# Fused attention and gated convolution FFN: convolution weights prepared at the start, the whole kernel in program order

## The chip, the cores and the metric

The kernel runs on one core of a Trainium2 chip. The metric is the device time of one execution in microseconds (us), the median over several executions. Engine names as in the profile: PE is TensorE (matmuls; PEld its weight loads), DVE is VectorE, ACT is ScalarE, POOL is GpSimd, SP is SyncE. The last two mostly issue transfers here.

## The reference

Eight batches, eight heads, 576 positions, head size 64. Linear attention with a root-mean-square norm, then an FFN whose hidden layer is gated by a convolution over the positions:

```python
kv  = einsum('bhsd,bhse->bhde', k, v)
out = einsum('bhsd,bhde->bhse', q, kv)
x   = out / sqrt(mean(out*out, -1) + 1e-6) * g_norm        # heads side by side: 512 columns
h   = maximum(x @ w_in, 0)                                 # 512 -> 1024
c[s] = cw[0]*h[s-1] + cw[1]*h[s] + cw[2]*h[s+1]            # per column of h, zero beyond the ends
y   = (h * sigmoid(c)) @ w_out                             # 1024 -> 512
```

The change concerns cw, the 3 x 1024 weights of the convolution (moe_conv_w).

## The kernel before

Batches are worked in five groups: batch 0, batch 1, and then three pairs. For each batch, k, v and q are loaded by POOL's queue as bf16, the first batch in two parts (six heads, two heads). For a batch, PE multiplies k by v (kv_mm, line 397) into a bank of PSUM; VectorE or ScalarE copies the result out (kv_out, line 351 or 349); q is transposed on PE (tr_mm, line 460) and copied out as qT; the product of qT and kv (line 371) gives `ot_ps`. ScalarE squares it, PE sums the squares (ss_mm, line 538), ScalarE takes Ln and Exp of the sums, PE spreads them over the columns (rb_mm, line 660 in the first group), and VectorE multiplies (x_mul, lines 671 and 678) to give xT. Then come `h` (line 785), the convolution and `o` (line 737).

The convolution is done in two ways. For the first group and some later parts it runs on PE with three diagonal matrices `diag` per column block (cw_diag, line 966, one VectorE instruction for each of the three taps). Elsewhere VectorE and ScalarE use weights relative to the middle tap, `cw_rel`, which cw_ratio (lines 973 to 980) makes in eight small VectorE instructions. Both start from `cw`: the 24 x 128 rows `cw_rows` come in by SP (line 286), PE transposes them in fp32 into `cw_ps` (cw_mm, line 959), VectorE copies them to `cw` (cw_out, line 962).

PSUM tiles come from two pools: three of two banks (`ps_two`) and two of one bank (`ps_one`). kv_ps, qT_ps, ss_ps and cw_ps, and at the start warm_ps and spread_ps, take turns in `ps_one`: each waits until the tile before the last has been read.

The order of the work has two parts. Everything ahead of the plan, lines 233 to 317, is put in order by a scheduler of the tile framework. The main part consists of numbered operations (class Plan), and the string ORDER lists them in the order in which they are issued; the letter behind a number chooses the engine (a is ScalarE, d is VectorE), and `*n` puts n filling matmuls of ones ahead of the operation (function `fill`, line 359) that keep PE running. This part runs under `tc.manual_schedule()` (line 1045), which keeps the order as written. Each engine works its queue strictly in order. The operations of kind LAND only stand for the time at which something is expected.

At the start PE runs warming matmuls of ones (line 242): `warm(14)` before the loads are issued, `warm(22)` behind the transposes that make `spread` (lines 301 to 306). `ident`, the identity matrix that transposes need, is made on POOL between the first transfer issues; `sel`, `neg`, `spread` and `spread32` are small constants for the sums and the spreading. The scheduler has put all 36 warming matmuls in one block ahead of the transposes, and the third load (q) between the two instructions that make ident.

Of the kernel before, what the change touches and what calls it, by code (L numbers as in the profile page):

```python
# [25 lines left out]
def _patch_pnc_remap() -> None:  # L26
# [28 lines left out]
FP32 = mybir.dt.float32  # L55
# [18 lines left out]
PARTS = (3, 1)  # L74
NORM_TABLES = "natural_log_exp_and_others"
ORDER = """
    103 8 11 0 7 17*7 18d 9 19*6 20a 24 21*2 29 25d 26 104 22 30d 27 31*4 32 12 10 34*1 35d 36*1 23a
    37d 33d 41*1 42 38*1 1 43*2 40d 105 13 39 49*2 50 28d 44 2 47*2 106*4 48 6 107a 108 53*2 45*2 54
    3 114*1 109*1 110a 115a 51*1 124 125a 46 119 120a 52 55 64 56a 4 5 65d 111 112 116 117 126 127
    113d 118d 205 212 217 68 128a 121 14 122 66 213d 218a 204 69d 123d 129 130 59 60d 222 82 131 67  # L80
    86 83a 87d 203 70 71 72 57 58 84 85 132 133 223a 134 135 209 210a 138 136 137 208 227 61 139
    228d 62 63 88 89 90 140 141a 148a 235 236d 144 145a 150a 206 146 240 147d 151d 142 143d 149d
    241a 211 214 216a 207 215 367 152 153 154d 157d 155d 156d 158 170 15 164 171a 165a 229 231a 219
    230 232 233a 234 168 169a 73 74d 172d 250 251d 77 78d 75 221a 245 16 159 220 175a 374 79 76 80
    246d 375d 174d 378 379d 81 160 166 167d 242 243 247 249a 248 365 366 94 252 224 173d 244d 176
    177 179d 181d 180d 178d 95a 237 238 225 253 100 101a 226d 382 383d 368 255 256 369 182 96 257 91
    371*1 372d 239a 254a 184 373 258*4 259 185 92a 272*2 273 268*2 269 264*2 265 262*1 263 186 370
    390*1 391a 162 93 260*1 266*1 161 183 386*1 267 270 271 261 97 98a 376 384 377 187 274 393 276
    387a 385 388 389 163 200 394a 288 275d 277d 290d 278 280 279d 289d 281d 201a 392 405 406d 401
    291d 402a 282 523 283a 284 285a 292d 525 532 533d 403 404 524 407 408 397 398d 286 544 545d 380  # L90
    526 527 287a 293d 294 295 296d 299d 298d 297d 300 528 399 400 381 529 530a 531 395 306 320 396
    409 410 411 316 307a 317a 548 549a 202 102 550 321a 412 413 414 415 308 309a 322d 314 315a 324d
    301 318 319d 325d 310 536 311a 551 552d 537d 312 313d 326 559 560a 323d 555*1 556d 327 330d 331d
    328d 329d 538 534 539 332 546 535 540 553 554 541a 561 547 562 194 563 564a 195a 196 99 542 543
    557 558 565 566 188 189a 418 416 567 568 417 336 304 335 424 419 569 425 302 197 303 420 421 190
    422 423 191 192a 193 430 431 428 429 432 433d 444 445a 570 426 427 440 334 305 434 435a 448d
    441a 436 437d 333 337 438 439a 449d 198a 199 446 447a 451d 442 443a 450a 452 453 454d 466 464
    465a 470 467a 471a 457d 455d 359 360a 456a 458 480d 476 477a 478 472 473a 479a 468 571 572 573
    361 469a 481d 483d 474 475a 484 575 482d 485 486d 362 350 462 363a 351a 364 352 459 353 354a 355
    576 577 578 586 579 489a 460 344 345a 461 487d 488d 490 574 590 584 587 591 341 342a 493 347  # L100
    348a 349 346 585 494 492 343 338 580 588 581 582 583 356 589 491 592 593a 598 599a 596 597a 463
    339a 340 600d 622 623a 603d 495 594 595a 604 601a 602d 605 608d 606d 607d 609d 610 646 618 620
    647a 621a 616 617a 624d 627d 619a 628 644 626d 645a 357a 625d 629 631d 630d 632d 613 633d 634
    611 640 358 641a 642 502 643a 614 503a 504 612 648d 650d 649d 615 652 651d 653 654d 656d 655d
    657d 658 520 666 521a 635 522 505 637 506a 507 667a 499 500a 501 517 678 664 638 636 639 665a
    518a 519 668d 669d 687 670 671 659 673d 508 679a 509a 660 672d 510 511 512d 513 661 674 514 662
    702 663 515a 516 680d 676 703a 681 704 682 683d 684 675 677 688a 690 689d 691 692d 696 693 697a
    685 698 699 686 700a 705 701 706d 707 694 695 496 497d 498 708 709a 710 711 717 712a 713 714
    718a 719 715a 716 720 721a 722
"""  # L110
NF = 4
GROUPS = ((0,), (1,), (2, 3), (4, 5), (6, 7))
# [82 lines left out]
def kernel(  # L195
# [11 lines left out]
    nc = tc.nc  # L207
# [3 lines left out]
    P = 128  # L211
# [5 lines left out]
    n_ff = D_ff // P  # L217
# [4 lines left out]
    consts = pool("consts", 1)  # L222
# [7 lines left out]
    ps_two = pool("ps_two", 3, space=PSUM)  # L230
    ps_one = pool("ps_one", 2, space=PSUM)

    nc.scalar.preload_act_table_set(NORM_TABLES)


    ones = consts.tile([P, 288], BF16, name="ones")
    nc.vector.memset(ones, 1.0)
    warm_ps = ps_one.tile([P, 288], FP32, name="warm_ps", tag="one")

    def warm(n):  # L240
        for _ in range(n):
            nc.tensor.matmul(warm_ps, ones[:, :P], ones, start=True, stop=True)  # L242

    warm(14)


# [12 lines left out]
    ident = consts.tile([P, P], BF16, name="ident")  # L259
# [17 lines left out]
    def load_w_out(half):  # L277
        fs = slice(half * n_ff // 2, (half + 1) * n_ff // 2)
        nc.gpsimd.dma_start(
            out=w_out_sb[:, fs, :], in_=moe_w_out.rearrange("(f p) m -> p f m", p=P)[:, fs, :])  # L280

    g_sb = consts.tile([P, 1], FP32, name="g_sb")
    for i in range(2):
        nc.sync.dma_start(out=g_sb[i * D:(i + 1) * D, :], in_=g_norm.unsqueeze(1))
    cw_rows = consts.tile([3 * n_ff, P], FP32, name="cw_rows")
    nc.sync.dma_start(out=cw_rows, in_=moe_conv_w.rearrange("k (f p) -> (k f) p", p=P))
    ident32 = consts.tile([3 * n_ff, 3 * n_ff], FP32, name="ident32")
    nc.vector.tensor_copy(ident32, ident[:3 * n_ff, :3 * n_ff])
    eps_sb = consts.tile([P, 1], FP32, name="eps_sb")
    nc.vector.memset(eps_sb, eps)  # L290

# [4 lines left out]
    for c in range(4):  # L296
        for i in range(2):
            nc.vector.memset(
                sel[i * D:(i + 1) * D, c, :24].rearrange("p (w m) -> p w m", m=8)[
                    :, :, 2 * c + i:2 * c + i + 1], 1.0)  # L300
    spread_ps = ps_one.tile([P, 4, P], BF16, name="spread_ps", tag="one")
    for c in range(4):
        for t in range(n_hd):
            nc.tensor.transpose(spread_ps[t * SM:(t + 1) * SM, c, :], sel[:, c, :], ident)
    spread = consts.tile([P, 4, P], BF16, name="spread")
    nc.vector.tensor_copy(spread, spread_ps)
    warm(22)

    spread32 = consts.tile([P, 2, P], FP32, name="spread32")
# [10 lines left out]
    plan = Plan()  # L320
# [3 lines left out]
    def ring(name, bufs):  # L324
        return rings.setdefault(name, Ring(bufs))


    TWO, ONE = ring("two", 3), ring("one", 2)
# [4 lines left out]
    def one_bank(shape, dtype, name):  # L333
        return ps_one.tile(shape, dtype, name=name, tag="one")
# [615 lines left out]
            g.o_ops.append(om)  # L950


    cw = consts.tile([P, 3, n_ff], FP32, name="cw")
    cw_rel = consts.tile([P, 3, n_ff], FP32, name="cw_rel")
    cst = {}

    def cw_mm():
        cst["ps"] = one_bank([P, 3 * n_ff], FP32, "cw_ps")
        nc.tensor.transpose(cst["ps"], cw_rows, ident32)

    def cw_out():
        nc.vector.tensor_copy(cw.rearrange("p k f -> p (k f)"), cst["ps"])

    def cw_diag(j):

        nc.vector.tensor_mul(
            diag[:, j, :, :], ident.unsqueeze(1).to_broadcast([P, n_ff, P]),
            cw[:, j, :].unsqueeze(2).to_broadcast([P, n_ff, P]))
# [10 lines left out]
        for j in (0, 2):  # L979
            nc.vector.tensor_mul(cw_rel[:, j, :], cw[:, j, :], sgn[:, 1, :])  # L980

    landed = plan.op("LAND", 9.0, None)
    mm = plan.op("PE", 0.3, cw_mm, deps=[landed])
    cw_done = plan.op("DVE", 0.2, cw_out, deps=[mm])
    Hold(ONE, mm, [cw_done])
    diag_done = []
    if any(map(any, C_PE)):
        diag = consts.tile([P, 3, n_ff, P], BF16, name="diag")
# [22 lines left out]
    for g in groups:  # L1011
        g.by_act, g.by_dma, g.x_from, g.kv_from = (c[g.n] for c in (BY_ACT, Q_DMA, X_FROM, KV_FROM))
        for b in g.bs:
            for name, src in (("k", k), ("v", v), ("q", q)):
                if b > 0:
                    need = []
                    if b > 1:
# [4 lines left out]
                        deps=[load_ops[name, b - 1]] if b > 1 else [])  # L1022
# [19 lines left out]
            tails([(groups[0], 0), (groups[1], 0)])  # L1042
    for g in groups:
        Hold(ring("h", 2), g.h0[0], g.o_ops)
    with tc.manual_schedule():
        for o in plan.order():
            if o.fn is not None:
                o.fn(*o.args)
# [1 line left out]
_INS = ['q', 'k', 'v', 'g_norm', 'moe_w_in', 'moe_conv_w', 'moe_w_out']  # L1050
_OUTS = [((8, 576, 512), 'float32')]
# [25 lines left out]
```

## Time and profile before

| what | value |
|---|---|
| time, median of 13 runs | 200.5 us (199.8 to 203.86) |
| the profiled execution's own time | 200.6 us |
| its span | 198.8 us |
| TensorE busy | 188.4 us (95%) |
| VectorE busy | 153.2 us (77%) |
| ScalarE busy | 139.1 us (70%) |
| transfers | 31.49 MB, mean 158 GB/s |

The profile is of one execution. The difference of 1.8 us between its time and its span lies around the instructions, before the first and after the last. Busy times are sums over one engine; the chain is followed back from the last instruction, at each step to the one that released it. The timeline gives instructions of an engine in order of time, merged where alike.

### The profile page before, as it was taken

To read this page: it belongs to the slowest core of one execution; us is meant where nothing else is said; L and a number is where in the kernel's file an instruction comes from. 1 tells how busy PE (TensorE), PEld (TensorE's weight loads), DVE (VectorE), ACT (ScalarE), POOL (GpSimd) and SP (SyncE) were. 2 spreads that over 40 slices of the span, in tenths; PEclk is the share of its full clock that TensorE was granted. 3 is DMA by queue.
4 is the path that set the end of the run, shared out by engine and by line. 5 is a ranking of instruction groups with operands and counts; after the bars stand their busy time and mean duration, and the time that the engine had idled before them with its cause. 6 is when DMAs were issued, how large, how long until landed. Compare 5 with 4: busy or idle time off the path is not lost.

```text
span 198.8 us, 4703 instructions
## 1 busy us (share of the span) xinstructions
PE 188.4 (95%) x1899; PEld 118.2 (59%) x1910; DVE 153.2 (77%) x281; ACT 139.1 (70%) x211; POOL 40.5 (20%) x61
## 2 busy tenths in 40 slices
PE   7999989999989989999999999999999999999990
PEld 4765566886854555777854477654457754644440
DVE  2127777897979866769999999999989999978200
ACT  2046068878969976288897998788988788677131
POOL 7706040013323114011000699110000000000000
PEclk9999999999999999999999999999999999999998
DMA  4999999997999999998689721398542034354653
GB/s 50 198 203 206 203 206 205 203 206 119 140 195 204 226 216 211 205 162 106 177 192 231 218 54 53 111 264 201 145 141 73 0 112 119 86 150 131 166 148 99
DMA packets 32714, 31.49 MB, mean 158 GB/s; under 512 B 2332, under 2 KB 28084, under 8 KB 32692
## 3 DMA queue, kind: packets, MB, share of 16 engines
q0 software_dynamic: 20976, 16.25, 53.9%
q1 hardware_dynamic: 11716, 14.93, 28.6%
q8 instruction: 15, 0.25, 0.5%
q14 instruction: 7, 0.06, 0.1%
HBM read 37.24 MB, written 9.73 MB: 236 GB/s over the span
## 4 chain that ended last, share of the span: by engine, by line
PE 70%; DVE 10%; DMA 9%; ACT 6%; issue 1%; POOL 0%; DVEq 0%; ACTq 0%
PE o_ps L737 27%; PE h_ps L785 20%; DMA v_sb<-in_v_dram 6%; PE ot_ps L371 4%; PE warm_ps L242 3%; DMA kv_sb<-kv_sb 3%; DVE tap L853 3%; PE qT_ps L460 3%; PE kv_ps L397 2%; PE c_ps L825 2%; DVE conv L875 2%; DVE conv L873 2%; PE rb_ps L660 2%; PE o_ps L928 2%; ACT qT L349 2%; DVE h L884 2%
## 5 line engine op out<-in xcount | busy, mean ns | idle before, releaser
L785 PE MATMUL h_ps<-xT,w_in_sb 128*128 128x288 bf16 x512 | 67.4, 286 | 0.4 <-DVE h L798 0.3
L737 PE MATMUL o_ps<-w_out_sb,h 128*128 128x512 bf16 x261 | 60.5, 379 | 0.6
L785 PEld LDWEIGHTS <-w_in_sb 128*128 128x128 bf16 x512 | 48.6, 98 | 15.0 <-issue 2.2
L737 PEld LDWEIGHTS <-h 128*128 128x128 bf16 x272 | 25.7, 98 | 30.6 <-issue 1.4
L879 ACT ACTIVATE conv<-conv,cw_rel 128x576 bf16<-128x576 bf16 (+1 forms) x40 | 37.1, 962 | 1.5 <-DVE conv L875 1.3
L796 ACT ACTIVATE h<-h_ps 128x576 bf16<-128x576 f32 x46 | 28.9, 648 | 8.4 <-PE h_ps L785 8.2
L853 DVE TENSOR_SCALAR tap<-h,cw_rel 128x576 bf16<-128x576 bf16 (+1 forms) x73 | 29.7, 449 | 2.4 <-ACT h L796 1.3
L349 ACT ACTIVATE o_sb<-o_ps 128x512 f32<-128x512 f32 x33 | 19.7, 596 | 15.5 <-PE o_ps L737 9.7
L483 ACT ACTIVATE sq<-ot_ps 128x576 bf16<-128x576 f32 x32 | 19.6, 655 | 4.2 <-PE ot_ps L371 3.7
L884 DVE TENSOR_TENSOR h<-h,conv 128x1152 bf16<-128x1152 bf16 (+3 forms) x16 | 22.0, 1380 | 0.6 <-ACT conv L834 0.5
L864 POOL COPY conv<-h 128x4 bf16<-128x4 bf16 (+3 forms) x12 | 3.9, 324 | 89.4 <-ACT h L796 31.6
L875 DVE TENSOR_TENSOR conv<-conv,tap 128x1152 bf16<-128x1152 bf16 (+11 forms) x36 | 20.4, 622 | 1.1
L873 DVE TENSOR_TENSOR conv<-h,tap 128x1152 bf16<-128x1152 bf16 (+11 forms) x36 | 20.3, 620 | 0.9 <-ACT tap L851 0.4
L349 ACT ACTIVATE qT<-qT_ps 128x576 bf16<-128x576 bf16 x14 | 8.8, 649 | 16.0 <-PE qT_ps L460 16.0
L798 DVE TENSOR_SCALAR h<-h_ps 128x576 bf16<-128x576 f32 x18 | 13.3, 753 | 5.4 <-PE o_ps L928 2.7
L371 PE MATMUL ot_ps<-qT,kv_sb 64*64 64x288 bf16 x192 | 12.4, 297 | 2.0 <-ACT qT L349 0.6
L678 DVE TENSOR_TENSOR xT<-o,rb_ps 128x576 bf16<-128x576 f32 x15 | 10.6, 750 | 3.7 <-PE rb_ps L663 2.0
L254 POOL DMA_DIRECT2D q_sb<-in_q_dram x9 | 6.8, 751 | 30.9 <-PE qT_ps L460 25.7
L684 DVE SCALAR_TENSOR_TENSOR xT<-ot_ps,g_sb,rb 128x576 bf16<-128x576 f32 x16 | 12.2, 811 | 1.1 <-PE ot_ps L371 0.8
L460 PE MATMUL qT_ps<-ident,q_sb 96*128 96x96 bf16 x192 | 12.6, 206 | 0.1
L460 PEld LDWEIGHTS <-q_sb 96*128 96x128 bf16 x192 | 10.4, 97 | 2.6 <-issue 0.8
L371 PEld LDWEIGHTS <-kv_sb 64*64 64x64 bf16 x192 | 5.1, 104 | 9.4 <-issue 7.6
(76 smaller groups left out, 173.1 us busy)
## 6 DMA issues: line engine op xcount, KB each, us to landing
out_dram<-o_sb SPq DMA_DIRECT2D x24, 192.0 KB, 2.3
rb<-scr SPq DMA_DIRECT2D x16, 288.0 KB, 5.3
k_sb<-in_k_dram POOLq DMA_DIRECT2D x7, 576.0 KB, 11.5
v_sb<-in_v_dram POOLq DMA_DIRECT2D x7, 576.0 KB, 13.7
q_sb<-in_q_dram POOLq DMA_DIRECT2D x7, 576.0 KB, 12.4
out_dram<-o_sb SPq DMA_DIRECT2D x24, 128.0 KB, 2.3
out_dram<-o_sb SPq DMA_DIRECT2D x24, 64.0 KB, 2.0
w_in_sb<-in_moe_w_in_dram POOLq DMA_DIRECT2D x2, 512.0 KB, 15.2
```

The source lines that it names most:

```text
L349: nc.scalar.activation(dst, src, AX.Copy, scale=1.0 if scale is None else scale)
L371: nc.tensor.matmul(ps[i * D:(i + 1) * D, e, :HS], kv, g.qT[bi][es, 2 * t + i, :], start=True, stop=True)
L460: nc.tensor.transpose(ps[:, i, j * PS:(j + 1) * PS], q_sb[:, 2 * t + i, j * P:(j + 1) * P], ident[:PS, :PS])
L483: nc.scalar.activation(g.sq[bi, t], ust["ps"][:, :, :HS], AX.Square)
L737: nc.tensor.matmul(st["ps"][:n, :], g.h[:, f, t0:t0 + n], w_out_sb[:, f, :], start=(f == 0), stop=(f == n_ff - 1))
L785: nc.tensor.matmul(ps[:, e, :HS], w_in_sb[:, t, f * P:(f + 1) * P], g.xT[:, t, at:at + HS], start=(t == 0), stop=(t == n_hd - 1))
L796: nc.scalar.activation(dst, st["ps"][:, :, :HS], AX.Relu)
L853: nc.vector.tensor_scalar_mul(dst, src, cw_rel[:, j, f:f + 1])
L873: nc.vector.tensor_add(c[:, :, here], h[:, :, here], t[:, :, there])
L875: nc.vector.tensor_add(c[:, :, there], c[:, :, there], t[:, :, here])
L879: nc.scalar.activation(cst["c"][:, f - f0, :], cst["c"][:, f - f0, :], AX.Sigmoid, scale=cw_rel[:, 1, f:f + 1])
L884: nc.vector.tensor_mul(hs, hs, cst["c"])
```

## The change

The plan's operations for cw are removed (the transpose of cw_rows and its copy), which lowers every later number in ORDER by two. The transpose and the copy now stand in the part ahead of the plan, behind the copy of `spread` and ahead of `warm(22)`. `manual_schedule()` is entered at the start, so that the part ahead of the plan is issued as written too: 14 warming matmuls, the transposes for spread, the transpose of cw_rows, 22 warming matmuls; and on POOL ident is made ahead of the third load. On SP cw_rows is loaded ahead of g_sb. `warm` takes a bank of its own each time it is called, which makes the second block wait for the copy of spread.

In ORDER the ratio (4) and the three diagonals (1, 2, 3) come first, ahead of the first kv_mm; before, they stood between the operations of the first group's norm. Otherwise the order is the same, and only numbers of fills differ: with the new operation numbers, 15 (first kv_mm) 7 to 6, 17 and 22 (first two transposes of q) 6 to 7 and 0 to 1, 19 and 29 (first and third product) 2 to 1 and 4 to 3, 32 (second kv_mm) 1 to 0, 34, 36 and 39 (transpose, sums of squares, fourth product) 1 to 2 each, 41 and 47 (rb, sums) 2 to 3 each, 51 and 43 (rb) 2 to 4 and 2 to 3, 112, 107 and 122 (transposes of batch 1) 1 to 2, 1 to 2 and 0 to 1; later 256 4 to 3, 262 2 to 1, 268 0 to 1, 369 and 553 1 to 0.

```diff
 ORDER = """
-    103 8 11 0 7 17*7 18d 9 19*6 20a 24 21*2 29 25d 26 104 22 30d 27 31*4 32 12 10 34*1 35d 36*1 23a
-    37d 33d 41*1 42 38*1 1 43*2 40d 105 13 39 49*2 50 28d 44 2 47*2 106*4 48 6 107a 108 53*2 45*2 54
-    3 114*1 109*1 110a 115a 51*1 124 125a 46 119 120a 52 55 64 56a 4 5 65d 111 112 116 117 126 127
+    0 4 1 2 3 101 6 9 5 15*6 16d 7 17*7 18a 22*1 19*1 27 23d 24 102 20 28d 25 29*3 30 10 8 32 33d
+    34*2 21a 35d 31d 39*2 40 36*2 41*3 38d 103 11 37 47*3 48 26d 42 45*2 104*4 46 105a 106 51*4 43*3
+    52 112*2 107*2 108a 113a 49*1 122*1 123a 44 117 118a 50 53 62 54a 63d 109 110 114 115 124 125
...
+    ctx.enter_context(tc.manual_schedule())
     nc.scalar.preload_act_table_set(NORM_TABLES)
...
-    warm_ps = ps_one.tile([P, 288], FP32, name="warm_ps", tag="one")
 
     def warm(n):
+        warm_ps = ps_one.tile([P, 288], FP32, name="warm_ps", tag="one")
         for _ in range(n):
             nc.tensor.matmul(warm_ps, ones[:, :P], ones, start=True, stop=True)
...
+    cw_rows = consts.tile([3 * n_ff, P], FP32, name="cw_rows")
+    nc.sync.dma_start(out=cw_rows, in_=moe_conv_w.rearrange("k (f p) -> (k f) p", p=P))
     g_sb = consts.tile([P, 1], FP32, name="g_sb")
     for i in range(2):
         nc.sync.dma_start(out=g_sb[i * D:(i + 1) * D, :], in_=g_norm.unsqueeze(1))
-    cw_rows = consts.tile([3 * n_ff, P], FP32, name="cw_rows")
-    nc.sync.dma_start(out=cw_rows, in_=moe_conv_w.rearrange("k (f p) -> (k f) p", p=P))
     ident32 = consts.tile([3 * n_ff, 3 * n_ff], FP32, name="ident32")
-    nc.vector.tensor_copy(ident32, ident[:3 * n_ff, :3 * n_ff])
...
+    nc.vector.tensor_copy(ident32, ident[:3 * n_ff, :3 * n_ff])
     spread_ps = ps_one.tile([P, 4, P], BF16, name="spread_ps", tag="one")
...
     nc.vector.tensor_copy(spread, spread_ps)
+
+    cw = consts.tile([P, 3, n_ff], FP32, name="cw")
+    cw_rel = consts.tile([P, 3, n_ff], FP32, name="cw_rel")
+    cw_ps = ps_one.tile([P, 3 * n_ff], FP32, name="cw_ps", tag="one")
+    nc.tensor.transpose(cw_ps, cw_rows, ident32)
+    nc.vector.tensor_copy(cw.rearrange("p k f -> p (k f)"), cw_ps)
     warm(22)
...
-    cw = consts.tile([P, 3, n_ff], FP32, name="cw")
-    cw_rel = consts.tile([P, 3, n_ff], FP32, name="cw_rel")
-    cst = {}
-
-    def cw_mm():
-        cst["ps"] = one_bank([P, 3 * n_ff], FP32, "cw_ps")
-        nc.tensor.transpose(cst["ps"], cw_rows, ident32)
-
-    def cw_out():
-        nc.vector.tensor_copy(cw.rearrange("p k f -> p (k f)"), cst["ps"])
...
-    landed = plan.op("LAND", 9.0, None)
-    mm = plan.op("PE", 0.3, cw_mm, deps=[landed])
-    cw_done = plan.op("DVE", 0.2, cw_out, deps=[mm])
-    Hold(ONE, mm, [cw_done])
+    cw_done = plan.op("LAND", 6.2, None)
...
-    with tc.manual_schedule():
-        for o in plan.order():
-            if o.fn is not None:
-                o.fn(*o.args)
+    for o in plan.order():
+        if o.fn is not None:
+            o.fn(*o.args)
```

## The prediction

> **What bounds the kernel now.** I read the page first (busy shares, chain by engine), then the timeline of the first 30 us, where all edits lie, then the chain piece by piece, to see what carries a delay from there to the end.
>
> ```profile
> span 198.8 us, 4703 instructions
> PE 188.4 (95%) x1899; PEld 118.2 (59%) x1910; DVE 153.2 (77%) x281; ACT 139.1 (70%) x211; POOL 40.5 (20%) x61
> PE 70%; DVE 10%; DMA 9%; ACT 6%; issue 1%; POOL 0%; DVEq 0%; ACTq 0%
> ```
>
> TensorE (PE) is busy for 95% and holds 70% of the chain. Little idle time is left in which a delay could vanish.
>
> Timeline, first part (start, duration, engine, line, operation; in brackets the idle time before and what ended it):
>
> ```profile
> 1.23 6.91 PE L242 MATMUL warm_ps<-ones 128*128 128x288 bf16 x36 [1.23 <-DVE eps_sb L290]
> 4.34 0.36 DVE L314 TENSOR_REDUCE neg<-ident 128x1 f32<-128x96 bf16 x2
> 8.06 0.41 PE L304 MATMUL spread_ps<-ident,sel 128*32 128x128 bf16 x16
> 8.52 0.42 DVE L306 COPY spread<-spread_ps 128x512 bf16<-128x512 bf16 x1 [3.82 <-PE spread_ps L304]
> 8.98 0.48 DVE L316 SCALAR_TENSOR_TENSOR spread<-spread,neg 128x256 f32<-128x256 bf16 x1
> 9.37 1.33 PE L397 MATMUL kv_ps<-v_sb,k_sb 96*64 96x64 bf16 x72
> 10.74 0.56 DVE L351 CAST kv_sb<-kv_ps 128x384 bf16<-128x384 f32 x1 [1.27 <-PE kv_ps L397]
> 11.37 0.68 PE L460 MATMUL qT_ps<-ident,q_sb 96*128 96x96 bf16 x12
> 12.53 0.32 PE L371 MATMUL ot_ps<-qT,kv_sb 64*64 64x288 bf16 x4 [0.24 <-ACT qT L349]
> ...
> 23.44 1.22 DVE L966 TENSOR_TENSOR diag<-ident,cw 128x1024 bf16<-128x1024 bf16 x1
> 26.63 2.35 DVE L966 TENSOR_TENSOR diag<-ident,cw 128x1024 bf16<-128x1024 bf16 x2
> ```
>
> To see here: all 36 warming matmuls run in one block, though the program has 14, then the transposes, then 22. VectorE (DVE) waits 1.27 us for kv_ps and then empties it at once, by 11.30. The two transposes of q run in one go at 11.37, the second in the bank that this copy freed.
>
> The chain, piece by piece (start, duration, work):
>
> ```profile
> 17.12 1.16 PE rb_ps L660 x4
> 18.29 0.35 PE ss_ps L359 x2
> 18.64 0.35 PE ss_ps L538 x2
> 18.99 0.35 PE rb_ps L359 x2
> 19.34 1.16 PE rb_ps L660 x4
> 20.50 0.54 PE kv_ps L359 x4
> 21.04 0.97 PE kv_ps L397 x48
> 22.01 0.35 PE rb_ps L359 x2
> 22.36 0.68 PE rb_ps L660 x2
> ```
>
> From 17.1 to 25.4 it is PE after PE, with no wait of another engine between. L359 is the fill: matmuls of ones, put in where PE was planned to wait. Here they are on the path: two cost 0.35, four cost 0.54, so one more costs about 0.12. After that the chain stays on PE up to 49.4, goes by a k/v swap (51.54, 6.42 us) and the load of v_sb (59.62, 11.59 us) to 71.25, and on over PE. The load and the swap start when PE lets their issuer go, so a delay at 27 us goes through.
>
> **The change part by part.**
>
> *1. VectorE's queue.* Moved ahead of the first kv copy: the copy of cw (0.18), eight small operations of the ratio (21.21 to 22.70 in the timeline: 1.5) and three diagonals (1.22 + 2.35 = 3.57). neg (0.36) and spread32 (0.48) now also stand behind the spread copy. When does this start? The 20 warming matmuls up to 6.0 us are 0.24 apart (4.77 us / 20), the later ones 0.12. So 14 end at 1.23 + 3.4 = 4.6; ident is ready by about 3.5, as its mask no longer stands behind a 0.73 us issue on POOL. The 16 transposes took 0.41 at the quick rate; I take 0.8 for the slow one: 5.4. Copy of spread (0.42) to 5.9, cw to 6.1, neg 6.5, spread32 7.0, ratio 8.5, diagonals 12.0. kv_ps is complete at about 10.8; its copy runs from 12.0 to 12.56 instead of 10.74 to 11.30: 1.26 late.
>
> Who waits: the second transpose of q, for the bank of kv_ps. It starts at 12.7 instead of about 11.7; the first product, behind it on PE, at 13.15 instead of 12.53 (+0.6); the copy of the second qT (0.46) ends at 13.66, the next product comes 0.6 late. Then fills fall away (4 to 3 before the third product, 1 to 0 before the second kv), others come in before the sums of squares (1 to 2), and the Ln and Exp on ScalarE are some 0.45 late: rb starts at 17.5 instead of 17.05. **+0.45.** Bounds: if the clock is up from 4.6 on, DVE is free at 11.6 and +0.15 is left. The landing of cw_rows isn't shown; it is issued first now, at 0.74. The nearest rows are g_sb on the same queue (2.3 us) and, far slower, the swaps (5.1): landed at 3.0 or 5.8. I take the first, as the load traffic has hardly begun; the second adds 0.4 and gives +0.85.
>
> *2. Warming in program order.* The cw transpose and the 22 warmers wait: the transpose for cw_rows (the warmers, kv_mm and all else of PE queue behind it), the warmers for the copy of spread, whose bank they reuse: PE stands for some 0.4 us around 5.5. Then 22 x 0.12 = 2.7 and 6 fills (7 before), with 0.25 between: kv_mm at 9.5 instead of 9.37. v lands at 2.23 + 6.9 = 9.1 and q at 3.10 + 8.2 = 11.3 either way (q's issue moves about 0.3 back behind the mask, but k and v, 864 KB at 200 GB/s, keep the queue full beyond it). Within the cover of q: **0**, if the clock rises at 6.0 as before; the first rival if not.
>
> The Trainium skill (TensorE: Matmul & The Clock Gate, "What's actually happening") says that the array runs at half clock until it was busy for a whole window of about 3.4 us, the window running freely. The rows agree on the two rates (0.24 and 0.12), not on when: 4.8 us after the first matmul, which a free window allows. By that rule a gap around 5.5 could cost one window more, to about 9.4, and by an estimate from it kv_mm would start near 11.3, +2.6 us in all with the terms below; by the rows taken above it is 0.
>
> *3. Fills, numbers changed.* Between rb (17.5) and the second transpose of batch 1 there are 6 more: 1 before the second ss, 2 and 1 before the rb of the last part, 1 each before two transposes; another before the first rb hides in its wait for Exp, and one before the third transpose in the wait for its bank. 6 x 0.12 = **+0.7**. Bounds: 0, if PE by then waits for ScalarE or VectorE after all, and 0.72. I take the upper, since the chain shows no wait there. Later net 3 fewer, two of them around 65 to 72, ahead of the wait for v_sb (cover: that load, 11.59), and one further on: **-0.1** (0 to -0.36).
>
> *4. Taken away.* cw_ps on PE (16.39, 0.24): the next rb waited for Exp until 17.05, so 0 (at most -0.24). On VectorE 5.2 us between 19 and 29: every xT there ends a wait for rb on PE (1.30, 0.37, 0.91 idle), and after the last two diagonals (to 28.98) h waits for h_ps until 29.07; only the first diagonal ends 0.1 past its rb. 0 (at most -0.1). The copies of qT, 4 on ScalarE at 25.45, stay as they are. g_sb lands about 0.6 later, still 10 us before its first reader at 14.9.
>
> Sum: 0.45 + 0.7 - 0.1 = +1.05, say **+1.1**. The profiled execution took 200.6 (198.8 span and 1.8 around it), 0.1 over the median of 200.5: **201.7**. By the ends of the bounds: 0.15 + 0 - 0.7 = -0.55 to 0.85 + 0.72 = +1.6, so 200.0 to 202.2 is the likeliest's own range.
>
> **The rivals.**
>
> *A. The clock rises late (slower).* For: the gap around 5.5 falls into the 4.77 us that before were unbroken. Against: most of that time is still filled. If the count began anew at 5.95, 20 warmers run 0.24 apart to 10.7, the other 2 and 6 fills take 1.0, kv_mm starts at 12.0 with the hand-over: +2.6 there; less 0.2 for fewer fills, plus 0.7 - 0.1: +3.0, **203.6**.
>
> *B. No difference.* The copy's delay is eaten by fills, and the added fills stand in real waits. For: the fills are counted from planned waits. Against: the chain above. +0.2: **200.8**.
>
> *C. Faster.* At 51.54 a swap of 32 KB takes 6.42 us among the loads of w_out, k and v, and v_sb 11.59 after it. If a shift of PE against POOL lets the swap land like a 64 KB store (2.0), up to 4.4 come free, of which PE can use its waits there (0.72 and 0.83) and some of the fills and slack before 71.25: I put 3.1. Net of +1.1 that is -2.0: **198.6**. It counts as faster once the swap saves 2.1. Against: its issue and the loads move together.
>
> **How the numbers follow.** Likeliest 0.45, A 0.25, B 0.13, C 0.17. A measurement tells about 0.5% (1.0 us) from no change, so the bounds are 199.5 and 201.5. The likeliest lies just above: 0.30 slower, 0.15 same. Slower 0.30 + 0.25 = 0.55; same 0.15 + 0.13 = 0.28; faster 0.17. Range: from 199.5 (C below it, some 0.1 after its weaker half) to 204.0, over A's price.
>
> **What would show it.** Spread transposes near 4.7 and VectorE in one block from about 5.5 to 12; the kv copy ending near 12.5 with no wait for PE; a gap on PE before the second transpose; the first h_mm at 28.0 instead of 26.95 and from there all stages 1.1 late. Wrong if: warming matmuls stay 0.24 apart beyond 7 us (A); h_mm of the first group at or before 27.2 (B); the first h_mm late but the v_sb wait at 71.25 over earlier than now (C).

## The result, and the profile after

The changed kernel takes 202.89 us (median of 11 runs, 202.34 to 205.84) against 200.4 us for the kernel before (median of 48 runs shown with it). The ratio is 1.014, with a 95% interval of 1.0111 to 1.0170: slower by about 2.5 us, where the prediction had +1.1. Some executions of most kernels here, of the one before too, take 1 to 4 us longer, with a mean granted clock of TensorE of 0.98 to 0.99; the ratios leave most of them out, and no reading below rests on one unless it says so.

The profiled execution of the changed kernel took 202.31 us, the lowest time seen; that of before took 200.6. So the two traces are 1.7 us apart and can account for that much of the 2.5; the rest lies in executions without a trace. The head of its page, with the chain by engine:

```profile
span 200.5 us, 4719 instructions
PE 189.0 (94%) x1905; PEld 118.5 (59%) x1916; DVE 153.9 (77%) x281; ACT 139.0 (69%) x211; POOL 40.6 (20%) x61
PE 64%; DMA 14%; DVE 10%; ACT 5%; POOL 2%; issue 2%; SPq 0%; DVEq 0%; ACTq 0%; POOLq 0%
```

PE's share of the chain fell from 70% to 64%, and the transfers' rose from 9% to 14%. So something that PE waits for got later. The timeline of the changed kernel (start, duration, engine, line, operation, in brackets the idle time before and what ended it) shows where:

```profile
1.23 3.41 PE L243 MATMUL warm_ps<-ones 128*128 128x288 bf16 x14 [1.23 <-DVE eps_sb L290]
4.57 0.41 PE L305 MATMUL spread_ps<-ident,sel 128*32 128x128 bf16 x16
5.03 0.42 DVE L307 COPY spread<-spread_ps 128x512 bf16<-128x512 bf16 x1 [1.30 <-PE spread_ps L305]
5.50 2.85 PE L243 MATMUL warm_ps<-ones 128*128 128x288 bf16 x22 [0.36 <-DVE spread L307]
8.30 3.49 DVE L962 TENSOR_TENSOR diag<-ident,cw 128x1024 bf16<-128x1024 bf16 x3
10.35 1.33 PE L404 MATMUL kv_ps<-v_sb,k_sb 96*64 96x64 bf16 x72 [1.26 <-DMA v_sb<-in_v_dram]
11.72 0.56 DVE L358 CAST kv_sb<-kv_ps 128x384 bf16<-128x384 f32 x1
13.70 0.32 PE L378 MATMUL ot_ps<-qT,kv_sb 64*64 64x288 bf16 x4 [0.23 <-ACT qT L356]
...
18.45 1.23 PE L667 MATMUL rb_ps<-rs,spread 32*128 32x288 f32 x4
...
29.09 2.12 PE L792 MATMUL h_ps<-xT,w_in_sb 128*128 128x288 bf16 x16
```

The last two of these in the kernel before:

```profile
17.05 1.23 PE L660 MATMUL rb_ps<-rs,spread 32*128 32x288 f32 x4
26.95 2.12 PE L785 MATMUL h_ps<-xT,w_in_sb 128*128 128x288 bf16 x16
```

TensorE is ready for the first kv_mm at 9.1 and waits 1.26 us for v_sb; before, kv_mm ran at 9.37. The first product comes 1.17 later than before (13.70 against 12.53), the first rb 1.40 later, the first h_mm 2.14 later. VectorE does stand in its diagonals until 11.79, and its copy of kv_ps follows at once, as foretold; but as kv_ps was itself not complete before about 11.7, that queue cost almost nothing here.

Why v_sb was late is seen in the transfer rates, one row for each microsecond (window, its length, granted PE clock, mean DMA share, GB/s). First the kernel before:

```profile
5.00:6.00 1.00, 1.00 1.31 202
6.00:7.00 1.00, 1.00 1.30 191
7.00:8.00 1.00, 1.00 1.28 195
8.00:9.00 1.00, 1.00 1.33 203
```

The same rows of the changed kernel:

```profile
5.00:6.00 1.00, 1.00 0.96 129
6.00:7.00 1.00, 1.00 0.85 104
7.00:8.00 1.00, 1.00 1.19 160
8.00:9.00 1.00, 1.00 1.27 184
```

The changed kernel has a hole: 577 KB moved in these 4 us instead of 791. The missing 214 KB are 1.07 us at 200 GB/s. Every load of the first batch lands late, by 1.1 to 1.6 us, and the second part of q by 2.7: from issue to landing the first k takes 6.8 us (before 5.2), v 8.1 (6.9), q 9.0 (8.2, and it is issued 0.38 later), the second q 10.8 (8.1). Of the two transfers of g_sb the first takes 2.3 us, as before, and the second 5.9 instead of 2.4.

The chain of the changed kernel in order of time (start, duration, work):

```profile
5.47 10.78 DMA q_sb<-in_q_dram
...
23.53 0.60 PE rb_ps L366 x4
24.13 0.68 PE rb_ps L667 x2
24.81 0.47 PE rb_ps L366 x3
...
53.98 6.56 DMA kv_sb<-kv_sb
...
61.75 10.91 DMA v_sb<-in_v_dram
```

The second part of q, not the first v, is the transfer that lies on the chain; it lands at 16.25 and adds 0.2 us of wait before the sums of squares (rb is 1.40 late where the first product was 1.17 late). The fills (L366) stand on the chain with 4 and 3 where 2 and 2 stood. Further on the swap takes 6.56 us as before (6.42), and the load of v_sb behind it is 0.7 us shorter (10.91 against 11.59), so that of the 2.14 us at the first h_mm 1.46 are left at the end of that wait (72.71 against 71.25) and 1.70 at the last o.

### The profile page after: what moved, and what is told of

It is laid out like the page before. It is cut to its first block, busy times and chain, and to the rows that moved or that the text cites. A ratio compares the mean times of both kernels' runs of the same rounds, so it can differ in the third digit from the quotient of the medians.

```text
span 200.5 us, 4719 instructions
## 1 busy us (share of the span) xinstructions
PE 189.0 (94%) x1905; PEld 118.5 (59%) x1916; DVE 153.9 (77%) x281; ACT 139.0 (69%) x211; POOL 40.6 (20%) x61
## 3 DMA queue, kind: packets, MB, share of 16 engines
q0 software_dynamic: 20976, 16.25, 53.5%
## 4 chain that ended last, share of the span: by engine, by line
PE 64%; DMA 14%; DVE 10%; ACT 5%; POOL 2%; issue 2%; SPq 0%; DVEq 0%; ACTq 0%; POOLq 0%
PE o_ps L744 27%; PE h_ps L792 20%; DMA v_sb<-in_v_dram 5%; DMA q_sb<-in_q_dram 5%; DMA kv_sb<-kv_sb 3%; PE ot_ps L378 3%; DVE tap L860 3%; PE qT_ps L467 2%; PE rb_ps L667 2%; PE c_ps L832 2%; DVE conv L882 2%; DVE conv L880 2%; PE o_ps L935 2%; DVE h L891 1%; PE kv_ps L404 1%
## 5 line engine op out<-in xcount | busy, mean ns | idle before, releaser
L378 PE MATMUL ot_ps<-qT,kv_sb 64*64 64x288 bf16 x192 | 12.5, 298 | 2.0 <-ACT qT L356 0.6
## 6 DMA issues: line engine op xcount, KB each, us to landing
k_sb<-in_k_dram POOLq DMA_DIRECT2D x7, 576.0 KB, 11.8
```

The costliest lines, as they stand in the source:

```text
L378: nc.tensor.matmul(ps[i * D:(i + 1) * D, e, :HS], kv, g.qT[bi][es, 2 * t + i, :], start=True, stop=True)
```

## The experiments

Two theories were set up for the hole. **G**: the second transfer of g_sb, 64 elements of four bytes, is now the third transfer on SP instead of the second, and is moved among the first loads; that hinders them. **D**: the work brought forward on VectorE hinders them, by way of POOL, which issues the loads at that time. What SP issues in the kernel before:

```profile
0.74 1.22 SPq L284 DMA_DIRECT2D g_sb<-in_g_norm_dram  x2
2.00 0.59 SPq L286 DMA_DIRECT2D cw_rows<-in_moe_conv_w_dram  x1
```

and in the changed kernel:

```profile
0.74 0.43 SPq L284 DMA_DIRECT2D cw_rows<-in_moe_conv_w_dram  x1
1.23 1.20 SPq L287 DMA_DIRECT2D g_sb<-in_g_norm_dram  x2
```

So the second transfer of g_sb was issued by 1.96 us and is now issued from 1.83 to 2.43. The packets of SP's queue in the changed kernel between 5 and 6, 6 and 7, and 7 and 8 us (count, MB, share of the 16 engines' time):

```profile
q1 hardware_dynamic: 48, 0.00, 5.2%
q1 hardware_dynamic: 25, 0.00, 1.8%
q1 hardware_dynamic: 7, 0.00, 0.6%
```

By their count these are the 80 packets of g_sb's second transfer. In the kernel before all 160 packets of g_sb are moved ahead of 4 us.

### 1. g_sb ahead of cw_rows again

```diff
 changed kernel
+    [g_sb, two transfers on SP]
     cw_rows = ...; nc.sync.dma_start(out=cw_rows, ...)
-    [g_sb, two transfers on SP]
```

> The changed kernel with the two transfers of g_sb (128 elements of 4 bytes) issued ahead of cw_rows again, as before the change. Theory G (g_sb's tiny transfers, now issued beside the first k, stall the transfer engines from 5.1 to 8.5 us): the dip in GB/s from 5 to 8 us goes (200 instead of 83 to 170), v lands at about 9.1 instead of 10.35, the first k-by-v matmul starts at about 9.4, and the kernel is about 1.0 to 1.2 us faster than the changed one (some 201.3 to 201.7). Theory D (VectorE's work on the convolution weights, 5.4 to 11.8 us, keeps POOL from preparing its transfers): the dip stays, v lands at 10.3, time within 0.4 us of the changed kernel (202.3 to 202.9).

The hole is gone (199, 185 and 197 GB/s between 5 and 8 us), and v lands 6.9 us after its issue. But now cw_rows lands late. Timeline:

```profile
5.95 0.21 PE L312 MATMUL cw_ps<-ident,cw_rows 24*128 24x24 f32 x1 [0.85 <-DMA cw_rows<-in_moe_conv_w_dram]
12.43 0.55 DVE L358 CAST kv_sb<-kv_ps 128x384 bf16<-128x384 f32 x1
13.03 0.28 PE L366 MATMUL qT_ps<-ones 128*128 128x288 bf16 x1 [0.86 <-DVE kv_sb L358]
```

TensorE stands 0.85 us for cw_rows at 5.95, VectorE starts its block later and reaches the kv copy at 12.43, and TensorE waits 0.86 for the bank that this copy frees. First rb 18.11, first h_mm 28.75. By the time the expectation was missed: the traced execution took 201.74 us, but the median is 203.66 and the ratio 1.0204 (1.0150 to 1.0257, four runs); two others ran at a full clock and took 203.35 and 203.97, and where they lost more no trace shows. The trace shows the prediction's first step, visible once v is on time: rb is 1.06 us late, somewhat past the upper bound of 0.85 that was put there for a late cw_rows. Whoever stands third on SP is served late: cw_rows here, with its 24 rows of 512 bytes, without a hole; g_sb's four-byte elements in the changed kernel, with one.

### 2. VectorE's work where it was

```diff
 ORDER of the changed kernel
-    0 4 1 2 3 101 6 9 5 15*6 ...   104*4 46 105a ...   52 112*2 ...   54a 63d
+    0 101 6 9 5 15*6 ...   104*4 46 4 105a ...   52 1 112*2 ...   54a 2 3 63d
```

> The changed kernel with the ratio and the three diagonals moved back to the places in the plan that they had before the change; cw itself is still transposed and copied at the start, g_sb still behind cw_rows. Theory D: the two long operations of the ratio (0.56 and 0.53 us instead of 0.17) are gone from 6.3 to 7.7 us and the dip with them, v lands near 9.1, about 1.0 to 1.2 us faster than the changed kernel (201.3 to 201.7). Theory G: the dip from 5.1 us stays and v lands at about 10.3; time within 0.4 us of the changed kernel, as VectorE was free just in time there. If only part of the dip goes, both have a share.

The hole stays (113, 114 and 157 GB/s), v takes 8.4 us, and kv_mm starts at 10.69, again upon v_sb. D falls. This rests on the trace, whose granted clock is 1.00 up to 72 us; the times, 202.90 and three of 205.76 to 205.91 (ratio 1.0245, 1.0176 to 1.0314), lie too far apart to tell.

### 3. The fills of before

```diff
 ORDER of the changed kernel, the first rows (the later fills were put back too)
-    15*6 ... 17*7 18a 22*1 19*1 ... 29*3 ... 32 33d 34*2 ... 39*2 ... 36*2 41*3 ... 47*3
+    15*7 ... 17*6 18a 22 19*2 ... 29*4 ... 32*1 33d 34*1 ... 39*1 ... 36*1 41*2 ... 47*2
-    51*4 43*3 52 112*2 107*2 ... 122*1
+    51*2 43*2 52 112*1 107*1 ... 122
```

> The changed kernel with the numbers of filling matmuls of the kernel before (9 fewer ahead of the first h, 3 more later). My term for fills (6 on the path, 0.12 us each): the first h of batch 0 starts about 0.7 us earlier against rb (10.0 instead of 10.6 us after the first rb matmul's start at about 18.4), the kernel some 0.6 to 0.8 us faster than the changed one (202.0 to 202.3). If fills stand in real waits (rival B): no difference, within 0.2 us. The dip and v's landing at 10.3 stay as they are.

From the first rb to the first h_mm it takes 9.89 us (18.33 to 28.22), as before (9.90), against 10.64 in the changed kernel: the added fills are 0.75 us. The hole stays (129, 98, 148). 201.84 us (foretold 202.0 to 202.3), ratio 1.0094 (1.0057 to 1.0132).

### 4. The kernel before with cw_rows first on SP

```diff
 kernel before
+    cw_rows = ...; nc.sync.dma_start(out=cw_rows, ...)
     [g_sb, two transfers on SP]
-    cw_rows = ...; nc.sync.dma_start(out=cw_rows, ...)
```

> The kernel before with nothing changed but the order on SP: cw_rows ahead of the two transfers of g_sb. Theory G: the dip appears here too, GB/s falls to about 80 to 130 between 5 and 7 us, v lands at about 10.3, and the kernel is 0.9 to 1.2 us slower than before (201.3 to 201.7). Theory D: no dip, v at 9.1, time as before (200.2 to 200.6).

Nothing but this order was changed. The rates in the same windows as above:

```profile
5.00:6.00 1.00, 1.00 1.08 135
6.00:7.00 1.00, 1.00 0.81 95
7.00:8.00 1.00, 1.00 1.15 157
```

and its timeline:

```profile
10.40 1.33 PE L397 MATMUL kv_ps<-v_sb,k_sb 96*64 96x64 bf16 x72 [0.51 <-DMA v_sb<-in_v_dram]
18.28 1.23 PE L660 MATMUL rb_ps<-rs,spread 32*128 32x288 f32 x4
28.18 2.12 PE L785 MATMUL h_ps<-xT,w_in_sb 128*128 128x288 bf16 x16
```

The hole is there, rb and h_mm are 1.23 us late, and the time is 201.81 us, ratio 1.0086 (1.0057 to 1.0114). The wait is 0.51 and not 1.26, because TensorE came to kv_mm later in this execution (the 36 warming matmuls took 7.37 us, 6.91 in the traced one of before); v_sb sets the start either way. G holds: two lines exchanged on SP are more than half of the loss.

### 5 and 6. g_sb issued by ScalarE, and then VectorE's work late as well

```diff
 changed kernel (5)
+    g_sb = ...
+    for i in range(2):
+        nc.scalar.dma_start(out=g_sb[i * D:(i + 1) * D, :], in_=g_norm.unsqueeze(1))
     nc.scalar.preload_act_table_set(NORM_TABLES)
...
     cw_rows = ...; nc.sync.dma_start(out=cw_rows, ...)
-    [g_sb, two transfers on SP]
 (6): besides, 4, 1, 2, 3 in ORDER as in experiment 2
```

> The changed kernel with one thing different: the two transfers of g_sb are issued by ScalarE ahead of its table load, so that cw_rows is still first on SP and g_sb is not behind it. Theory G (the 128 four-byte elements of g_sb, put behind cw_rows, are moved among the first loads and cost 1.2 us of loading) says: the transfer rate stays near 200 GB/s between 5 and 8 us, v_sb lands at about 9.1, kv_mm starts at about 9.5. Then the step of the prediction on VectorE's queue comes to light: the first kv copy has to wait for the three diagonals until about 11.8 to 12.0, first product at 12.9 to 13.1, rb at 17.4 to 17.5, and with the added fills the first h_mm at 28.1; time 201.3 to 201.6. If instead the early work on VectorE and ScalarE slows the loads, the dip stays, kv_mm is at 10.35 and the first h_mm at 29.1, 202.5 to 202.9.

> The kernel with g_sb issued by ScalarE, and also the eight small operations of the ratio and the three diagonals at the places they had before the change. Difference to the kernel with g_sb by ScalarE alone is the price of VectorE's queue: the prediction put it at 0.45 us. Expected: the first kv copy at about 10.9 waiting for PE, rb at 17.1, first h_mm at 27.7 to 27.8, time 200.9 to 201.2. If VectorE's queue costs nothing, rb is the same in both kernels, within 0.1 us.

Both transfers of g_sb are now issued by 1.92 us, and cw_rows is first on its queue. The hole is gone (196, 190, 203 GB/s) and kv_mm starts at 9.37 in both. Timeline of the first kernel:

```profile
8.29 3.49 DVE L962 TENSOR_TENSOR diag<-ident,cw 128x1024 bf16<-128x1024 bf16 x3
11.70 0.55 DVE L358 CAST kv_sb<-kv_ps 128x384 bf16<-128x384 f32 x1
12.89 0.32 PE L378 MATMUL ot_ps<-qT,kv_sb 64*64 64x288 bf16 x4
```

and of the second:

```profile
10.74 0.56 DVE L358 CAST kv_sb<-kv_ps 128x384 bf16<-128x384 f32 x1 [4.17 <-PE kv_ps L404]
12.65 0.32 PE L378 MATMUL ot_ps<-qT,kv_sb 64*64 64x288 bf16 x4 [0.23 <-ACT qT L356]
```

With VectorE early, the kv copy is 0.96 late and the first product 0.24; rb (17.38 against 17.14) and the first h_mm (28.00 against 27.77) keep that difference. So the queue on VectorE costs 0.24 us by the traces. By the times it is 202.16 (foretold 201.3 to 201.6) against 201.16, ratios 1.0105 (1.0050 to 1.0160, five runs) and 1.0041 (1.0020 to 1.0062): 1.0 us. In the two profiled executions 0.7 us more come about at 72 us, where the first waits 0.75 us for v_sb and the second doesn't. The kernel of experiment 7 has VectorE's work late too and waits 0.67 us at that place, so the wait doesn't come with the early work alone. What the early work on VectorE costs in the whole time, 0.24 or up to 1.0 us, stays open.

The Trainium skill (DMA: Bandwidth & Descriptors, "Issuing engines are not separate DMA queues") says that issuing on a further engine saves only the issuer's time, as all transfers share the same 16 engines, and that this time is usually small beside the transfer. The rows agree: g_sb's two issues take 1.20 us on SP, about 0.6 each, beside 2.3 us to landing, and all that the second engine did was to make them earlier. But the size of the time saved doesn't tell its worth here: 0.5 us earlier for the second transfer was worth the whole hole of 1.07 us in other transfers.

### 7. All three undone

```diff
 as (6), and the fills of before as in experiment 3
```

> The same with the fills of the kernel before as well: all three suspected causes undone, with the program order, the early copy of cw and the warming in two blocks left in. If the three causes are all, the first h_mm is at 27.0 and the time that of the kernel before, 200.2 to 200.5. If something else of the change costs time, as the warming in two blocks or the cw transpose, the first h_mm stays later than 27.3.

200.43 us against 200.48 for the kernel before, ratio 0.9997 (0.9977 to 1.0018). The program order, the early cw, the warming in two blocks and the transpose of cw_rows are all still in it. So within the interval of 0.4 us they cost nothing, and the three causes are all there is: g_sb behind cw_rows, the queue on VectorE, and the fills. In its profiled execution (201.24, its second longest) the first h_mm is at 27.71 and not at 27.0: the clock rose later there, as the second block of warmers took 3.50 us instead of 2.85, which is 0.65 of the 0.7; rb to h_mm takes 9.89 there too. By the medians, the steps from 202.89 by way of 202.16 and 201.16 to 200.43 are 0.73, 1.00 and 0.73. By the traces they are 1.2, 0.24 and 0.75. The sums (2.46 and 2.2) agree better than the parts. One reason is that the loads hide the queue in the changed kernel, so that undoing g_sb alone gained 1.09 and not 1.2 at the first h_mm (29.09 to 28.00); it doesn't explain the 1.00 for the queue.

### 8, 9 and 10. The kernel before with fewer fills

If one fill costs 0.12 us, the fills of before between 18 and 26 us should be a cost as well.

```diff
 ORDER of the kernel before; 8: both rows, 9: the second and third alone, 10: the first alone
-    49*2 50 28d 44 2 47*2 106*4 48 6 107a 108
+    49 50 28d 44 2 47 106 48 6 107a 108
-    53*2 45*2 54
-    3 114*1 109*1 110a 115a 51*1
+    53 45 54
+    3 114 109 110a 115a 51
```

> The kernel before with 15 fills left out between 18 and 26 us (two each ahead of operations 49, 47, 53 and 45, four ahead of 106, one each ahead of 114, 109 and 51). If each fill there is on the path at 0.12 us, as the reading of the chain has it, the first h_mm comes 1.5 to 1.8 us earlier, at 25.2 to 25.5, and the time is 198.6 to 199.2. If the loads bind behind them (v of batch 1, q of batch 1, w_in), only 0.8 to 1.2 us are gained, or PE's clock falls and nothing is.

It got slower: 201.98 us, ratio 1.0103 (1.0035 to 1.0171). The windows of TensorE tell why (window, its length, busy time with the count of instructions, granted clock, DMA share, GB/s):

```profile
18.00:19.00 1.00, 1.00 (x6) 1.00 1.33 204
19.00:20.00 1.00, 1.00 (x6) 1.00 1.29 201
20.00:21.00 1.00, 1.00 (x39) 0.84 1.33 214
21.00:22.00 1.00, 1.00 (x21) 0.50 1.28 199
28.00:29.00 1.00, 1.00 (x6) 0.50 1.23 205
```

The clock falls to half at about 20.8 us and stays there until about 30.9; two rb with nothing before them take 1.3 us instead of 0.75, 16 h matmuls 4.0 instead of 2.1. The traced execution has a mean clock of 0.968; the other three have 0.963 and twice 0.983, and where the clock fell in them is on no trace. The Trainium skill (TensorE: Matmul & The Clock Gate, "Why this matters for your kernels") gives as the rule that the clock falls after some 3 us of idle TensorE. No such idle time is in these rows: the profile shows TensorE busy throughout. What ran there were rb matmuls of 32 rows in fp32 and few others. The measurement decides: for the clock, "busy" in the profile, whose ends of matmuls are modelled, is not enough. Whether the fills between those matmuls kept it up, and which, is asked by leaving out a part of them.

> The kernel before without the 7 fills that stand between 21.9 and 25.4 us (two each ahead of operations 53 and 45, one each ahead of 114, 109 and 51); the 8 between 18.2 and 21.0 stay. In the kernel without all 15, PE's clock fell to half from about 20.8 to 29.1 us, though PE had no idle time there. If the clock falls because of what PE did in the stretch before 20.8, it stays up here, the 7 fills are 0.85 us of pure cost, the first h_mm is at 26.1 and the time 199.4 to 199.8. If the fills of 22 to 25 are needed themselves, the clock falls to half somewhere between 24 and 30 and the time is 201 to 203.

> The other half: the kernel before without the 8 fills between 18.2 and 21.0 us (two each ahead of operations 49 and 47, four ahead of 106). If the fall of the clock at 20.8 comes from this stretch alone, it falls here too and the time is 201.3 to 202.6. If it takes both stretches to be thin, the clock stays up, 0.96 us are gained at the first h_mm (26.0), and the time is 199.3 to 199.8.

Without the 7 late fills the clock stays up: 199.81 us against 200.36, ratio 0.9960 (0.9928 to 0.9992), a mean clock of 0.993 or more in eight of ten executions, 0.986 and 0.985 in two. The first h_mm comes at 25.54, 1.41 us earlier than before, more than the 0.85 of the fills: six rb with nothing between them take 1.24 us, where two and four with fills between took 0.75 and 1.23. But by the medians only 0.55 of it lasts to the end. The chain of this kernel goes by another swap:

```profile
23.04 5.13 DMA kv_sb<-kv_sb
28.17 0.04 issue
28.21 0.33 PE ot_ps L371 x2
```

and after it h_mm waits for VectorE's o until 30.11 (30.93 before).

Without the 8 early fills, three of seven executions had a clock of 0.994 and took 199.6 to 199.8 us (ratio of these 0.9969, 0.9955 to 0.9984; first h_mm at 26.05 in the traced one); four had 0.961 to 0.969 and took 203.7 to 205.5. A mean clock below 0.97 is seen with the early fills left out alone: in two of four executions of experiment 8 and four of seven here, in none of the ten of experiment 9, and in none of the kernel before run beside them (0.981 or more). So by the count of executions the early fills hold the clock, though not every execution needs them, and the late ones are a cost alone. What decides in an execution is not shown. In the traced one here the clock rose earlier at the start than in that of experiment 8 (36 warming matmuls in 6.04 against 7.41 us), so the moment of the rise is a rival that no run tests.

### 11. Half of g_sb late

```diff
 changed kernel
+    nc.scalar.dma_start(out=g_sb[:D, :], in_=g_norm.unsqueeze(1))      (ahead of the table load)
     cw_rows = ...; nc.sync.dma_start(out=cw_rows, ...)
-    [g_sb, two transfers on SP]
+    nc.sync.dma_start(out=g_sb[D:2 * D, :], in_=g_norm.unsqueeze(1))
```

> The changed kernel with the first of the two transfers of g_sb issued by ScalarE and only the second left on SP behind cw_rows: 64 four-byte elements there instead of 128. If each element beside the loads costs its share, half the loading time is lost: the rate between 5 and 8 us has about half the hole, v_sb lands at about 9.7, kv_mm starts at 9.8 to 10.0, first h_mm 28.4 to 28.6. If the hole is made by any late transfer of this kind, whatever its size, kv_mm is at 10.35 and the first h_mm at 29.1. If only what is issued after 1.9 us falls among the loads (this transfer is issued at about 1.3 to 1.9, as the second one was before the change), the hole is gone, kv_mm is at 9.4 and the first h_mm at 28.0.

The hole is gone: 199, 185 and 198 GB/s between 5 and 8 us, v lands 6.8 us after its issue, and no packet of g_sb is moved after 4 us. Its issue on SP runs from 1.23 to 1.81, a little ahead of the time that the second transfer of g_sb had in the kernel before (1.38 to 1.96). So it isn't the company of cw_rows nor a share for each element: what SP had issued by 1.96 us was moved before 4 us, ahead of most of the loads, and what it issued behind that (g_sb from 1.83 to 2.43 in the changed kernel, cw_rows from 2.00 to 2.59 before) was moved among them. What makes that difference no run shows. 201.65 us, ratio 1.0060 (1.0041 to 1.0079), whose interval overlaps that of experiment 5. The first h_mm is at 28.28 and not at 28.0: the second block of warmers took 3.37 us, 0.5 more than in experiment 5.

### 12. The early work on VectorE without the late fills

```diff
 changed kernel with g_sb by ScalarE and the fills of before, less the seven of experiment 9
```

> The changed kernel (program order, cw, ratio and diagonals early on VectorE) with g_sb issued by ScalarE, the fills of the kernel before, and of these the 7 between 21.9 and 25.4 us left out that the kernel before could do without. It asks whether the early work on VectorE is worth anything once PE is not held up by fills there. Without those fills the kernel before started h_mm at 25.5 and stood at 28.2 for the swap of kv_sb and at 30.1 for an o by VectorE, behind 3.6 us of diagonals. If VectorE bound there, the h of the second batch now starts 0.4 to 0.6 earlier than 30.1 and the time is 199.0 to 199.4. If the swap (5.1 us from its issue behind kv_mm of batch 1) binds, the early work gains nothing and what it costs ahead of the first kv copy (0.24 between the two kernels with g_sb by ScalarE) is lost: 199.8 to 200.2.

```profile
28.07 0.76 DVE L806 TENSOR_SCALAR h<-h_ps 128x576 bf16<-128x576 f32 x1 [2.52 <-PE h_ps L793]
```

VectorE now stands idle for 2.52 us where its diagonals were, and nobody is the better for it: the swap (5.05 us from 23.63) ends at 28.69, and h_mm of the second batch starts at 30.64, 0.53 later than in experiment 9, as kv_mm of batch 1 was 0.55 later here (21.56 against 21.01; the clock rose later in this execution, too). 199.99 us, ratio 0.9964 (0.9936 to 0.9992): no better than experiment 9, as the swap binds.

## Why the prediction was right and wrong

The direction was right and the size too small, 1.1 against 2.5 us. Of the 1.1 only the 0.7 of the fills is in the 2.5; the 0.45 of VectorE's queue lay hidden behind a larger delay that wasn't foreseen. By its own steps:

**1. VectorE's queue (+0.45, bounds 0.15 to 0.85).** The mechanism was right: VectorE in one block from 5.0 to 11.8 (foretold 5.5 to 12), the copy of kv_ps without a wait for PE, and, in experiment 5, TensorE's wait of 0.38 for it ahead of the second transpose of q. The size was 0.24 by the traces with v on time, in the lower half of the bounds (up to 1.0 by the times, which stays open); with cw_rows late, that wait was 0.86. In the changed kernel itself it lay beside the wait for v_sb and cost about nothing.

**2. Warming, and with it the loads (0). This is the step that failed:** "v lands at 2.23 + 6.9 = 9.1 and q at 3.10 + 8.2 = 11.3 either way". v landed at 10.3 and q at 12.5. The step looked at when POOL issues the loads, which hardly changed (q alone, 0.38 later), and not at what else is under way on the same transfer engines. In step 4 the prediction did see that g_sb comes later, and costed that by its first reader alone, ten microseconds on. It put that transfer 0.6 us later; the trace has it land 4.0 us later (issue 0.45 later, and 5.9 us instead of 2.4). Nobody waits for g_sb; but its 64 elements of four bytes, issued from 1.83 us on, cost the loads 1.07 us, and TensorE 1.2 (experiment 4). So the term for the loads was 1.2 us and was put at 0.

**3. Fills (+0.7, the upper end taken).** Right: 0.74 in the changed kernel, 0.75 in experiment 3. The price of 0.12 each doesn't follow from the two rows it names, which give (0.54 - 0.35) / 2 = 0.095; the chain of the changed kernel, with 0.35, 0.47 and 0.60 for two, three and four fills of the same width, gives 0.12 to 0.13.

**4. Taken away (0), and fewer fills later (-0.1).** The 0 was right: with the fills of before, rb to the first h_mm takes 9.89 us in experiment 3 and 9.90 in the kernel before, though VectorE's work is gone from there. The -0.1 was not tested apart. That the chain stays on PE up to 49.4 was read too simply: it passes ScalarE at 25.45 (1.20 us) and 29.37 (0.66) and VectorE at 30.06 (0.83), which had no part in the miss. The freed time of VectorE has no taker even when the fills are gone (experiment 12).

The sum with the one term mended: 1.2 for the loads, 0.2 for the second part of q, 0 for VectorE's queue behind them and 0.75 for the fills are 2.15, and 2.14 were seen at the first h_mm. (The 0.2 is of this execution: the second q took 9.3 us in experiment 3, without such a wait.)

**The rivals.** A (a late clock) didn't come about: the second block of warmers ran about 0.12 us apart from 5.50 on. In other executions with this start the block lasted 3.3 to 3.5 us instead of 2.85, and the 36 warmers of the kernel before's start lasted 6.04 to 7.41 us (experiments 10 and 8). So the moment of the rise moves between executions, in the kernel before too, but no trace shows the loss of 2.6 us that A asked for. B (no difference) was wrong, as the fills are on the path. C (a shorter swap) was wrong in its size: the swap took 6.56 us; only the load of v_sb behind it gave 0.7 back.

## What to carry to other kernels

When a transfer is moved on a queue, look not only at who waits for it but at what it will be moved beside: here a tiny transfer of four-byte elements that slipped from before the bulk loads to among them cost a microsecond of loading, and issuing it on an idle queue was the remedy. Matmuls put in to fill the time are not free where the chain has no wait, yet in this kernel some of them hold the clock: take them away in groups and look at the granted clock each time, and not at the busy share. And work moved off a stage is worth something only if that stage waits for its engine; read there what else is waited for before paying for the move.

## What was not expected of the hardware

- The 80 packets that carried 64 four-byte elements took the transfer engines only a few per cent of their time by the count of packets (5.2, 1.8 and 0.6% in the three microseconds), and yet the engines' mean share fell from 1.31 and 1.30 to 0.96 and 0.85 (above 1, as packets overlap). So the engines had less under way, not more; what held them back no run here shows. A transfer of 24 rows of 512 bytes in the same place left no hole; whether it is the size of the elements or their number that matters was not tested apart.
- Two of the eight small operations of the ratio took 0.56 and 0.53 us in the changed kernel instead of 0.17. At that time POOL issued loads (6.09 to 7.66). This recurs in experiments 1 (0.45 and 0.52) and 5 (0.41 and 0.32, of which one was another operation), and is absent at the place they had before. Only operations of the form TENSOR_SCALAR were slowed, never the TENSOR_TENSOR or RECIPROCAL between them. Its cause was not tested.
- The clock of TensorE fell in the middle of a stretch in which the profile shows TensorE busy without a gap (experiment 8, at 20.8 us), and not in every execution: with the first eight fills left out, three of seven kept a mean clock of 0.994.
